# Dealing the last weights to chosen DMA engines, one output transfer, and a later load of x, in a one-core decode kernel

## The chip, the core and the metric

The kernel runs on one core of a Trainium2 chip. The core has a matrix engine (PE, with its weight loads shown apart as PEld), a vector engine (DVE), an activation engine (ACT), GpSimd (POOL) and a sync engine (SP) that here only issues transfers. Sixteen DMA engines move data between HBM and the on-chip memory (SBUF, 128 partitions). A transfer is issued by an instruction on SP or ACT; it is cut into packets, and a completion semaphore counts up as its engines finish.

The metric is device time in microseconds of one execution, the median of several runs. Less is better.

## What is computed

Two queries (batch of 2, one token) go through an attention block with a long cache and through a small feed-forward block, and a sigmoid gate mixes the two:

```python
g = sigmoid((x * gate_w).sum(-1))            # x: 2 x 1 x 512
q = x @ wq                                   # 512 -> 32 heads x 128
p = softmax(q . k_cache / sqrt(128))         # 2 x 32 heads, 4096 keys each
a = (p @ v_cache) @ wo                       # 4096 -> 512
b = relu(x @ w1) @ w2                        # 512 -> 1376 -> 512
out = g * a + (1 - g) * b                    # 2 x 1 x 512, bf16
```

All inputs are bf16. The two caches are 67 MB each; wq and wo are 4 MB each, w1 and w2 1.4 MB each. Every byte is read once.

## The kernel before

The program is written by hand: for each engine a list of instructions in order, with waits on counters of the other engines (`waits`) and on transfers' semaphores (`dwaits`). A wait holds everything behind it on that engine.

**Transfers.** SP issues nearly all of them, in this order: wq (4 MB); then the caches in 32 units of 4 MB, first four K units, then K and V in turn, then the last four V units (V12 to V15), each into one of three slots of `kv` as the unit that held the slot is done with (`freed`). Behind the third K unit stands w1 (L267), which goes into the place of wq and so waits for `pe_q`, the end of the projection of q. Behind V15 come the last weights: the last 96 rows of w2 in eleven transfers (L268 and L269, cut by `W2A` into 14, 13, 12, 11, 10, 9, 8, 7, 6, 4 and 2 rows of 1 KB); wo in two halves of 2 MB (L270, L271); the first 1280 rows of w2 in three pieces (L272, L273; 512, 512 and 256 KB). The output leaves in two transfers of 1 KB (`out_row`, L274 and L275), row 0 from SP (L277) and row 1 from ACT (L508); SP waits for both (L278). ACT issues x and gate_w (L259, L260) as its first two instructions.

**Front.** PE transposes x and gate_w (L283), DVE copies them (L286, L288, L289), PE makes the gate's sum (L293) and then q (L320), DVE and ACT spread q out (L333 to L351). POOL meanwhile sets constants: `ones32`, `ident16`, `xTw` (L219), `qbuf` (L220), others, and last `ptm` (L241). 

**Body.** For each of 64 quarter-units of K, DVE turns it (L380) and PE multiplies (L396). Each 16 of them close a softmax group; POOL copies its result into `ptm` (L425, waits for `c_ptm`), PE multiplies with V (L442), DVE collects (L453, L456). The feed-forward's hidden row `hT` is made once in between (L361, L367, L370).

**End.** After V15, PE gathers (L472, L480), DVE writes `oW` (L483), and `project` and `ffn_f` (both by `fin_row`, L488) accumulate the output in PSUM: for each of 32 rows of wo and 11 of w2 four products of 128 columns, one into each band of 32 output partitions, two partitions used in each. wo's first half is waited for at r = 0, its second at r = 16; then w2's last 96 rows, and its three pieces. DVE copies the result to `out_sb` (L507), and the two output transfers take partitions 0, 32, 64, 96 and 1, 33, 65, 97.

Of the kernel before, what the change touches and what calls it, by code (L numbers as in the profile page):

```python
# [3 lines left out]
dt = mybir.dt  # L4
# [8 lines left out]

NSLOT = 3
NKT = 3
W2A = ((0, 14), (14, 27), (27, 39), (39, 50), (50, 60), (60, 69), (69, 77), (77, 84), (84, 90), (90, 94), (94, 96))


class _Marker:
# [67 lines left out]
def bass_gated_mix__gqa_block_cached__dense_activation_relu__decode_kernel(  # L87
# [33 lines left out]
    wreg = sb("wreg", [128, 16384], dt.bfloat16)  # L121
    w2 = sb("w2", [128, 11, 512], dt.bfloat16)
# [18 lines left out]
    s4 = sb("s4", [32, 4, 128], dt.bfloat16)  # L141
    X2 = sb("X2", [128, 2, 8, 128], dt.float32)
    O_sb = sb("O_sb", [32, 2, 128], dt.bfloat16)
    oW = sb("oW", [128, 32, 2], dt.bfloat16)
    hT = sb("hT", [128, 11, 2], dt.bfloat16)
    out_sb = sb("out_sb", [128, 128], dt.bfloat16)

    PSF = nc.alloc_psum_tensor("PS", [128, 4096], dt.float32)
# [4 lines left out]
    def psf(p0, p1, c0, n):  # L153
        return PSF[p0:p1, c0:c0 + n]
# [8 lines left out]
    H_C0 = MISC + 72  # L163
    L_C0 = MISC + 96
    O_C0 = MISC + 128
    R_C0 = MISC + 256
    FIN_C0 = 0
# [4 lines left out]
    sem = {n: nc.alloc_semaphore("sem_" + n) for n in names}  # L172
# [29 lines left out]
    def pool(fn, waits=(), signal=None):  # L202
        P.add("pool", fn, waits=[marker(w) for w in waits], signal=marker(signal) if signal else None)

    def dve(fn, waits=(), signal=None, dwaits=()):
        P.add("dve", fn, waits=[marker(w) for w in waits], signal=marker(signal) if signal else None, dwaits=dwaits)

    def act(fn, waits=(), signal=None, dwaits=()):
        P.add("act", fn, waits=[marker(w) for w in waits], signal=marker(signal) if signal else None, dwaits=dwaits)

    def pe(fn, waits=(), signal=None, dwaits=()):
        P.add("pe", fn, waits=[marker(w) for w in waits], signal=marker(signal) if signal else None, dwaits=dwaits)
# [5 lines left out]
         waits=["c_i16z"], signal="c_i16")  # L218
# [13 lines left out]
         waits=["c_s1"], signal="c_s2")  # L232
    pool(lambda g: g.affine_select(out=sell[:, 16:32], in_=sell[:, 16:32], pattern=[[8, 4], [32, 4]],
                                   compare_op=ALU.is_ge, fill=0.0, base=7, channel_multiplier=-1),
         waits=["c_s2"], signal="c_sell")
# [3 lines left out]
         waits=["c_s4z"], signal="c_s4")  # L239
    pool(lambda g: g.memset(selx[:], 0.0), signal="c_selx")  # L240
    pool(lambda g: g.memset(ptm[:], 0.0), signal="c_ptm")  # L241


    wq_in = A_wq.rearrange("(p t) n -> p (t n)", t=4)
    w1_in = B_w1.rearrange("(p t) f -> p (t f)", t=4)
    wo_in = A_wo.rearrange("(p r) n -> p (r n)", r=32)
# [9 lines left out]
    def sp(fn, waits=(), dwaits=()):  # L256
        P.add("sp", fn, waits=waits, dwaits=dwaits)

    act(lambda e: e.dma_start(x_sb[0:2, :], A_x.rearrange("b s d -> (b s) d")).then_inc(sem["x"], 16))  # L259
    act(lambda e: e.dma_start(x_sb[2:3, :], gate_w.rearrange("(o d) -> o d", o=1)).then_inc(sem["gw"], 16))  # L260
    sp(lambda e: e.dma_start(wreg[:, :], wq_in).then_inc(sem["wq"], 16))
    for n, what in enumerate(order):
        waits = [freed(order[n - NSLOT])] if n >= NSLOT else []
        sp(lambda e, what=what: e.dma_start(kv[:, slot_of(what), :], unit_in(what)).then_inc(sem_slot[slot_of(what)], 16),  # L264
           waits=waits)
        if n == 2:
            sp(lambda e: e.dma_start(wreg[:, 0:5504], w1_in).then_inc(sem["w1"], 16), waits=[marker("pe_q")])  # L267
    for p0, p1 in W2A:  # L268
        sp(lambda e, p0=p0, p1=p1: e.dma_start(w2[p0:p1, 10, :], B_w2[1280 + p0:1280 + p1, :]).then_inc(sem["w2a"], 16))  # L269
    sp(lambda e: e.dma_start(wreg[:, 0:8192], wo_in[:, 0:8192]).then_inc(sem["wo0"], 16), waits=[marker("pe_h")])  # L270
    sp(lambda e: e.dma_start(wreg[:, 8192:16384], wo_in[:, 8192:16384]).then_inc(sem["wo1"], 16))  # L271
    for name, r0, r1 in (("w2b", 0, 4), ("w2c", 4, 8), ("w2d", 8, 10)):  # L272
        sp(lambda e, name=name, r0=r0, r1=r1: e.dma_start(w2[:, r0:r1, :], w2a_in[:, r0:r1, :]).then_inc(sem[name], 16))  # L273
    def out_row(e, b):  # L274
        return e.dma_start(out[b:b + 1].rearrange("b s (c n) -> (b s c) n", n=128), out_sb[b::32, :]).then_inc(sem["out"], 16)  # L275

    sp(lambda e: out_row(e, 0), waits=[marker("dve_out")])  # L277
    sp(lambda e: e.wait_ge(sem["out"], 32))  # L278


    def gate():
# [82 lines left out]

    def ffn_relu():
        for b in range(2):
            dve(lambda v, b=b: v.tensor_scalar(out=hT[:, 0:10, b], in0=PSF[:, H_C0 + b:H_C0 + 20:2], scalar1=0.0,  # L367
                                               scalar2=gm[:, b:b + 1], op0=ALU.max, op1=ALU.mult),
                waits=["pe_h", "dve_gm"])
            dve(lambda v, b=b: v.tensor_scalar(out=hT[0:96, 10, b:b + 1], in0=psf(0, 96, H_C0 + 20 + b, 1), scalar1=0.0,  # L370
                                               scalar2=gm[0:96, b:b + 1], op0=ALU.max, op1=ALU.mult),
                waits=["pe_h", "dve_gm"], signal=f"dve_h{b}")

# [47 lines left out]
    def sm_spread(g):  # L421
        dve(lambda v: v.transpose(out=ET_sb[:, :], in_=E_sb[:, :]),  # L422
            waits=[f"act_exp{g}"] + ([f"pool_pt{g - 1}_3"] if g else []), signal=f"dve_et{g}")
        for hq in range(4):
            pool(lambda e, g=g, hq=hq: e.tensor_copy(  # L425
                out=ptm[32 * hq:32 * hq + 32, g % 2, :, :, :, hq, :],
                in_=ET_sb[32 * hq:32 * hq + 32, :].rearrange("p (r u a c) -> p r u a c", r=16, u=4, a=2)),
                waits=[f"dve_et{g}", "c_ptm"] + ([f"pe_v_{4 * g - 5}"] if g >= 2 else []), signal=f"pool_pt{g}_{hq}")


    def v_unit(v):
# [38 lines left out]
    def o_gather(b):  # L470
        for u in range(8):
            pe(lambda e, u=u, b=b: e.matmul(psf(0, 32, O_C0, 128), lhsT=selx[:, 28 - 4 * u:60 - 4 * u], rhs=X2[:, b, u, :],  # L472
                                            start=(u == 0), stop=(u == 7)),
               waits=[f"dve_x{8 * b + u}_3"] + ([f"dve_rinv{b}", "dve_selx"] if u == 0 else []),
               signal=(f"pe_O{b}" if u == 7 else None))
        dve(lambda v, b=b: v.tensor_scalar(out=O_sb[:, b, :], in0=psf(0, 32, O_C0, 128), scalar1=rinv[:, b:b + 1],
                                           scalar2=gb[0:32, b:b + 1], op0=ALU.mult, op1=ALU.mult),
            waits=[f"pe_O{b}", f"dve_rinv{b}", "dve_g"], signal=f"dve_O{b}")
        for dq in range(4):
            pe(lambda e, dq=dq, b=b: e.matmul(psf(0, 128, R_C0 + 32 * b, 32), lhsT=s4[:, dq, :], rhs=O_sb[:, b, 32 * dq:32 * dq + 32],  # L480
                                              start=(dq == 0), stop=(dq == 3), tile_position=(0, 0)),
               waits=([f"dve_O{b}", "c_s4"] if dq == 0 else []), signal=(f"pe_R{b}" if dq == 3 else None))
        dve(lambda v, b=b: v.tensor_copy(out=oW[:, :, b], in_=psf(0, 128, R_C0 + 32 * b, 32)), waits=[f"pe_R{b}"], signal=f"dve_oW{b}")  # L483


    def fin_row(r, first, last, lhsT, rhs, dw, waits, signal):
        for c in range(4):
            pe(lambda e, c=c: e.matmul(psf(32 * c, 32 * c + 2, FIN_C0, 128), lhsT=lhsT, rhs=rhs[:, c * 128:(c + 1) * 128],  # L488
                                       start=first, stop=last, tile_position=(0, 32 * c), skip_group_check=True),
               dwaits=(dw if c == 0 else []), waits=(waits if c == 0 else []), signal=(signal if c == 3 else None))  # L490

    def project():
        dve(lambda v: v.memset(psf(0, 128, FIN_C0, 128), 0.0), waits=["act_exp2"], signal="dve_fin0")
        for r in range(32):
            dw = {0: [(sem["wo0"], 16)], 16: [(sem["wo1"], 16)]}.get(r, [])
            fin_row(r, r == 0, False, oW[:, r, :], wreg[:, r * 512:(r + 1) * 512], dw,
                    ["dve_oW0", "dve_oW1", "act_exp3", "dve_fin0"] if r == 0 else [], None)

    def ffn_f():
        for n, r in enumerate([10, *range(10)]):  # L500
            m = 96 if r == 10 else 128
            dw = {10: [(sem["w2a"], 16 * len(W2A))], 0: [(sem["w2b"], 16)], 4: [(sem["w2c"], 16)], 8: [(sem["w2d"], 16)]}.get(r, [])
            fin_row(r, False, r == 9, hT[0:m, r, :], w2[0:m, r, :], dw, ["dve_h0", "dve_h1"] if n == 0 else [],
                    "pe_fin" if r == 9 else None)

    def store():
        dve(lambda v: v.tensor_copy(out=out_sb[:, :], in_=psf(0, 128, FIN_C0, 128)), waits=["pe_fin"], signal="dve_out")  # L507
        act(lambda e: out_row(e, 1), waits=["dve_out"])  # L508


    gate()
# [7 lines left out]
    for i in range(64):  # L519
# [7 lines left out]
        if i % 16 == 0 and i:  # L527
            g = i // 16 - 1
# [5 lines left out]
        if i >= 19 and i % 4 == 3:  # L534
            v = i // 4 - 4
# [50 lines left out]
```

## Time and profile before

| | |
|---|---|
| three runs | 347.56, 347.62, 348.02 us; median 347.62 |
| profiled execution | 347.98 us in all; span from first to last instruction 346.5 us |
| HBM read over the span | 145.43 MB, 420 GB/s |
| PE, DVE, ACT, POOL busy | 203.3, 182.4, 13.9, 20.9 us |
| waits of SP before a unit of the caches | 245.2 us for DVE, 28.4 us for PE |
| V15, last unit: issued, landed | 303.51, 329.09 us |

The span is what the profiler sees of the core's instructions; the time of the execution has 1.48 us more around it.

The trace also has every DMA packet, with queue, start, length and bytes. It has no engine number, but an engine's packets follow one another without a gap (each begins some 4 ns before the end of the one before), so the packets can be strung into sixteen chains. The eleven transfers of w2's last rows tell the chains apart: the chains hold 11, 11, 10, 10, 9, 9, 8, 7, 6, 5, 4, 3, 2, 1, 0 and 0 packets of 1 KB, just what comes about if a transfer of n rows (n up to 16) puts one row on each of the first n engines. So the chain with 8 such packets is engine 6, and so on; 0|1, 2|3, 4|5 and 14|15 are pairs that this does not separate. Ends of the work on each chain, in us from the start of the span, and the times at which a packet of another queue (an instruction fetch of 16 KB, or of 8 KB where marked) stood between its packets:

| engine | end of V15 | w2's last rows | wo, first half | wo, second half | last piece of w2 | fetch at |
|---|---|---|---|---|---|---|
| 0 or 1 | 326.36 | 326.90 | 332.62 | 337.49 | 340.70 | |
| 0 or 1 | 326.44 | 326.97 | 332.83 | 337.69 | 340.88 | |
| 2 or 3 | 326.18 | 326.66 | 332.20 | 337.07 | 340.28 | |
| 2 or 3 | 328.33 | 328.82 | 334.47 | 339.34 | 342.49 | 110.1, 299.3 (8 KB) |
| 4 or 5 | 326.36 | 326.79 | 332.36 | 337.23 | 340.44 | |
| 4 or 5 | 328.04 | 328.48 | 334.20 | 339.07 | 342.22 | 100.5 |
| 6 | 328.01 | 328.40 | 333.98 | 338.84 | 342.00 | 140.6 |
| 7 | 326.29 | 326.63 | 332.14 | 337.03 | 340.23 | |
| 8 | 326.77 | 327.07 | 332.18 | 337.06 | 340.27 | |
| 9 | 327.88 | 328.12 | 333.13 | 338.02 | 341.21 | 178.1 |
| 10 | 327.81 | 328.00 | 333.00 | 337.88 | 341.08 | 216.9 |
| 11 | 328.00 | 328.14 | 333.15 | 338.04 | 341.24 | 257.1 |
| 12 | 328.20 | 328.30 | 333.28 | 338.17 | 341.36 | 294.9 |
| 13 | 328.63 | 328.68 | 335.17 | 340.06 | 343.23 | 40.7, 333.0 |
| 14 or 15 | 328.13 | none | 333.13 | 338.01 | 341.21 | 70.3 |
| 14 or 15 | 326.83 | none | 331.94 | 336.82 | 340.04 | |

A semaphore's count shows some 0.4 us after the packet that ends the work: the last piece of w2 is complete for PE at 343.65. Packet lengths in the stream are 1213 ns for 32 KB, 612 for 16 KB, 159 for 4 KB, 84 for 2 KB, 46 for a row of 1 KB and 9 for the write to a semaphore.

### The profile page before, as it was taken

Reading aid. Unit: us, or ns where it says so; the run is one execution under the profiler, and the core shown is the slowest. Engines: PE = TensorE matmul, PEld = TensorE weight load, DVE = VectorE, ACT = ScalarE, POOL = GpSimd, SP = SyncE. Lnnn points to the kernel's source line nnn. Section 1 sums busy time; section 2 is a strip of 40 time slices with the busy share of each in tenths; the row PEclk is TensorE's granted clock in tenths of the full one; section 3 lists DMA queues with packets and bytes.
Section 4 is the critical chain, followed back from the end, with each engine's and each line's share of the span. In section 5 each row is a group of like instructions: output and inputs, shape, how many; then the busy total and the mean of one; then the engine's idle time right before and its main releaser. Section 6 shows DMA issues by size and latency. Waiting matters only on the chain.

```text
span 346.5 us, 3037 instructions
## 1 busy us (share of the span) xinstructions
PE 203.3 (59%) x1334; PEld 76.7 (22%) x1334; DVE 182.4 (53%) x177; ACT 13.9 (4%) x48; POOL 20.9 (6%) x36
## 2 busy tenths in 40 slices
PE   0419959773755729175855839074785839422283
PEld 0203333221211203021221313021421213110052
DVE  0848877990917356391918355391648367211120
ACT  1030000000000000000000000000000000000000
POOL 8400000020000000020000000020000000200000
PEclk9967978999685958789695969789696969666576
DMA  8999999999999999999999999999999999999993
GB/s 322 446 431 431 404 453 443 427 429 424 424 426 436 443 431 431 429 424 431 435 429 439 431 435 424 422 431 435 439 426 443 427 424 431 423 435 435 395 412 154
DMA packets 5842, 145.61 MB, mean 420 GB/s; under 512 B 739, under 2 KB 838, under 8 KB 1222
## 3 DMA queue, kind: packets, MB, share of 16 engines
q1 hardware_dynamic: 5816, 145.43, 98.1%
q8 instruction: 10, 0.16, 0.2%
q14 instruction: 2, 0.02, 0.0%
q10 hardware_dynamic: 14, 0.00, 0.0%
HBM read 145.43 MB, written 0.00 MB: 420 GB/s over the span
## 4 chain that ended last, share of the span: by engine, by line
DMA 70%; DVE 14%; PE 12%; SPq 2%; issue 1%; DVEq 0%
DMA kv<-in_A_k_cache_dram 53%; DVE kt L380 11%; DMA w<-in_B_w_dram 10%; PE PS L396 8%; DMA kv<-in_A_v_cache_dram 8%; PE PS L442 4%; SPq L269 1%; DVE X L456 1%; DVE mpad L406 1%; DVE ET L422 1%; PE PS L488 0%; SPq L264 0%; DVE X L453 0%; DVE mrow L408 0%; DVE mmax L409 0%
## 5 line engine op out<-in xcount | busy, mean ns | idle before, releaser
L396 PE MATMUL PS<-kt,qbuf 128*128 128x512 bf16 x512 | 149.8, 446 | 93.9 <-DVE kt L380 93.7
L380 DVE STREAM_TRANSPOSE kt<-kv 128x2048 f32<-128x2048 f32 x64 | 144.0, 2285 | 102.8 <-DMA kv<-in_A_k_cache_dram 102.2
L396 PEld LDWEIGHTS PS<-kt,qbuf 128*128 128x128 bf16 x512 | 50.5, 108 | 190.3 <-DVE kt L380 117.8
L442 PE MATMUL PS<-kv,ptm 128*16 128x512 bf16 x512 | 37.2, 442 | 23.0 <-DMA kv<-in_A_v_cache_dram 23.0
L425 POOL COPY ptm<-ET 32x512 bf16<-32x512 bf16 x16 | 9.7, 607 | 276.5 <-DVE ET L422 275.8
L442 PEld LDWEIGHTS PS<-kv,ptm 128*16 128x16 bf16 x512 | 12.8, 98 | 45.8 <-issue 35.7
L453 DVE TENSOR_SCALAR X<-PS,maskc 128x128 f32<-128x128 f32 x16 | 5.1, 319 | 30.9 <-PE PS L442 30.9
L456 DVE SCALAR_TENSOR_TENSOR X<-PS,maskc,X 128x128 f32<-128x128 f32 x48 | 16.8, 351 | 1.7
L351 ACT ACTIVATE qbuf<-PS 32x4 bf16<-32x4 bf16 x32 | 5.7, 178 | 110.7 <-PE PS L396 110.1
L417 ACT ACTIVATE E<-PS,negm 128x512 bf16<-128x512 f32 x4 | 2.7, 687 | 154.5 <-DVE negm L413 154.5
L472 PE MATMUL PS<-X,selx 128*32 128x128 f32 x32 | 5.3, 336 | 0.0
L283 PE MATMUL PS<-ident,x_sb 3*128 3x3 bf16 x4 | 0.3, 168 | 8.1 <-DMA x_sb<-in_gate_w_dram 8.1
L361 PE MATMUL PS<-xT,wreg 128*128 128x2 bf16 (+1 forms) x44 | 2.8, 200 | 3.6 <-DMA wreg<-in_B_w_dram 3.6
L472 PEld LDWEIGHTS PS<-X,selx 128*32 128x32 f32 x32 | 4.4, 142 | 1.9 <-issue 1.4
L286 DVE COPY xT<-PS 128x12 bf16<-128x12 bf16 x1 | 0.2, 169 | 8.4 <-PE PS L283 8.4
L488 PE MATMUL PS<-wreg,oW 128*2 128x128 bf16 x128 | 2.6, 242 | 3.4 <-DMA wreg<-in_A_wo_dram 3.0
L220 POOL MEMSET qbuf<- 128x5120 bf16 x1 | 4.4, 4370 | 0.0
L507 DVE CAST out_sb<-PS 128x128 bf16<-128x128 f32 x1 | 0.3, 291 | 7.6 <-PE PS L488 7.6
L288 DVE COPY xTw<-xT 128x8 bf16<-128x8 bf16 x1 | 3.9, 3862 | 0.0
L406 DVE TENSOR_REDUCE mpad<-PS 128x1 f32<-128x512 f32 x4 | 2.7, 676 | 2.1 <-PE PS L396 2.1
L361 PEld LDWEIGHTS PS<-xT,wreg 128*128 128x128 bf16 (+1 forms) x44 | 2.7, 161 | 4.1 <-DMA wreg<-in_B_w_dram 4.1
L289 DVE TENSOR_TENSOR xg<-xT 128x8 f32<-128x8 bf16 x1 | 3.6, 3629 | 0.0
(58 smaller groups left out, 40.5 us busy)
## 6 DMA issues: line engine op xcount, KB each, us to landing
kv<-in_A_k_cache_dram SPq DMA_DIRECT2D x16, 4096.0 KB, 26.2
kv<-in_A_v_cache_dram SPq DMA_DIRECT2D x16, 4096.0 KB, 18.7
wreg<-in_A_wq_dram SPq DMA_DIRECT2D x1, 4096.0 KB, 12.4
wreg<-in_A_wo_dram SPq DMA_DIRECT2D x2, 2048.0 KB, 29.9
wreg<-in_B_w_dram SPq DMA_DIRECT2D x1, 1376.0 KB, 27.3
w<-in_B_w_dram SPq DMA_DIRECT2D x2, 512.0 KB, 33.4
w<-in_B_w_dram SPq DMA_DIRECT2D x1, 256.0 KB, 33.9
x_sb<-in_A_x_dram ACTq DMA_DIRECT2D x1, 2.0 KB
```

Of the source, the lines that this page charges most:

```text
L220: pool(lambda g: g.memset(qbuf[:], 0.0), signal="c_qbuf")
L288: dve(lambda v: v.tensor_copy(out=xTw[:, :, 0:2], in_=xT), waits=["dve_xT", "c_xTw"], signal="dve_xTw")
L351: act(lambda a, out=out, src=src: a.activation(out=out, in_=src, func=ACT.Copy), waits=[f"pe_sc_{4 * uh + 3}"], signal=f"q_1_{uh}_{hq}")
L361: return e.matmul(psf(0, m, H_C0 + 2 * ft, 2), lhsT=cols, rhs=xT3[:, t, 0:2], start=(t == 0), stop=(t == 3))
L380: dve(lambda v: v.transpose(out=dst, in_=pairs[:, :, 32 * k:32 * k + 32, :]), waits=([f"pe_sc_{i - NKT}"] if i >= NKT else []), dwaits=([s ...
L396: pe(lambda e, j=j, pos=pos, c=c, cc=cc: e.matmul(psf(0, 128, (g % 2) * BANK, 512), lhsT=qbuf[:, u % 8, j, 32 - pos:160 - pos], rhs=kt16[: ...
L406: dve(lambda v, g=g: v.tensor_reduce(out=mpad[:, 0:1], in_=psf(0, 128, (g % 2) * BANK, 512), axis=AX.X, op=ALU.max), waits=[f"pe_sc_{16 * ...
L425: pool(lambda e, g=g, hq=hq: e.tensor_copy(out=ptm[32 * hq:32 * hq + 32, g % 2, :, :, :, hq, :], in_=ET_sb[32 * hq:32 * hq + 32, :].rearra ...
L442: pe(lambda e, n=n, t=t, a=a, r16=r16, grp=grp, u4=u4, rows=rows: e.matmul(psf(32 * t, 32 * t + 16, V_B * BANK, 512), lhsT=ptm[:, grp % 2, ...
L453: dve(lambda e, src=src, dst=dst: e.tensor_scalar(out=dst, in0=src, scalar1=maskc[:, 0:1], scalar2=None, op0=ALU.mult), waits=[f"pe_v_{v}" ...
L456: dve(lambda e, src=src, dst=dst, c=c: e.scalar_tensor_tensor(out=dst, in0=src, scalar=maskc[:, c:c + 1], in1=dst, op0=ALU.mult, op1=ALU.add),
L472: pe(lambda e, u=u, b=b: e.matmul(psf(0, 32, O_C0, 128), lhsT=selx[:, 28 - 4 * u:60 - 4 * u], rhs=X2[:, b, u, :], start=(u == 0), stop=(u ...
```

## The change

- The last 96 rows of w2 go in two transfers, of 92 and 4 rows, in place of eleven. 92 rows are dealt to four engines.
- wo's first half goes in three transfers in place of one: the first 4 KB of 104 partitions (dealt to 13 engines), the same of the other 24 partitions (12 engines), and the remaining 12 KB of all 128 partitions (16 engines). `project` waits for all three.
- `oW` and `hT` get 32 columns for each row, of which 0 and 16 are used and the rest stays zero; the products take 17 columns of weights, and the two batch rows land 16 partitions apart. The output then is every 16th partition of `out_sb` and leaves in one transfer from SP; ACT issues none.
- POOL sets `hT` and `oW` to zero behind `ptm`, and the copies into `ptm` wait for the last of these.
- ACT issues x, and with it gate_w, only when POOL has set `xTw`.

```diff
-W2A = ((0, 14), (14, 27), (27, 39), (39, 50), (50, 60), (60, 69), (69, 77), (77, 84), (84, 90), (90, 94), (94, 96))
+W2A = ((0, 92), (92, 96))
+WO_A = 2048
...
-    oW = sb("oW", [128, 32, 2], dt.bfloat16)
-    hT = sb("hT", [128, 11, 2], dt.bfloat16)
+    oW = sb("oW", [128, 32, 32], dt.bfloat16)
+    hT = sb("hT", [128, 11, 32], dt.bfloat16)
...
     pool(lambda g: g.memset(ptm[:], 0.0), signal="c_ptm")
+    pool(lambda g: g.memset(hT[:], 0.0), signal="c_hT")
+    pool(lambda g: g.memset(oW[:], 0.0), signal="c_oW")
...
-    act(lambda e: e.dma_start(x_sb[0:2, :], A_x.rearrange("b s d -> (b s) d")).then_inc(sem["x"], 16))
+    act(lambda e: e.dma_start(x_sb[0:2, :], A_x.rearrange("b s d -> (b s) d")).then_inc(sem["x"], 16), waits=["c_xTw"])
...
-    sp(lambda e: e.dma_start(wreg[:, 0:8192], wo_in[:, 0:8192]).then_inc(sem["wo0"], 16), waits=[marker("pe_h")])
+    for n, (p0, p1, c0, c1) in enumerate(((0, 104, 0, WO_A), (104, 128, 0, WO_A), (0, 128, WO_A, 8192))):
+        sp(lambda e, p0=p0, p1=p1, c0=c0, c1=c1: e.dma_start(wreg[p0:p1, c0:c1], wo_in[p0:p1, c0:c1]).then_inc(sem["wo0"], 16),
+           waits=([marker("pe_h")] if n == 0 else []))
...
-    def out_row(e, b):
-        return e.dma_start(out[b:b + 1].rearrange("b s (c n) -> (b s c) n", n=128), out_sb[b::32, :]).then_inc(sem["out"], 16)
-    sp(lambda e: out_row(e, 0), waits=[marker("dve_out")])
-    sp(lambda e: e.wait_ge(sem["out"], 32))
+    sp(lambda e: e.dma_start(out.rearrange("b s (c n) -> c (b s) n", n=128),
+                             out_sb[0::16, :]).then_inc(sem["out"], 16),
+       waits=[marker("dve_out")])
+    sp(lambda e: e.wait_ge(sem["out"], 16))
...
-            pe(lambda e, c=c: e.matmul(psf(32 * c, 32 * c + 2, FIN_C0, 128), lhsT=lhsT, rhs=rhs[:, c * 128:(c + 1) * 128],
+            pe(lambda e, c=c: e.matmul(psf(32 * c, 32 * c + 17, FIN_C0, 128), lhsT=lhsT, rhs=rhs[:, c * 128:(c + 1) * 128],
...
-            dw = {0: [(sem["wo0"], 16)], 16: [(sem["wo1"], 16)]}.get(r, [])
-            fin_row(r, r == 0, False, oW[:, r, :], wreg[:, r * 512:(r + 1) * 512], dw,
+            dw = {0: [(sem["wo0"], 48)], 16: [(sem["wo1"], 16)]}.get(r, [])
+            fin_row(r, r == 0, False, oW[:, r, 0:17], wreg[:, r * 512:(r + 1) * 512], dw,
...
-            fin_row(r, False, r == 9, hT[0:m, r, :], w2[0:m, r, :], dw, ["dve_h0", "dve_h1"] if n == 0 else [],
+            fin_row(r, False, r == 9, hT[0:m, r, 0:17], w2[0:m, r, :], dw, ["dve_h0", "dve_h1"] if n == 0 else [],
...
-        act(lambda e: out_row(e, 1), waits=["dve_out"])
```

The writes of `hT` (in `ffn_relu`) and of `oW` (in `o_gather`) go to column `16 * b` in place of `b`, and wait for the zeroing.

More of the change, by code (lines that the diff above doesn't have):

```diff
@@ L366, in ffn_relu @@
         for b in range(2):
-            dve(lambda v, b=b: v.tensor_scalar(out=hT[:, 0:10, b], in0=PSF[:, H_C0 + b:H_C0 + 20:2], scalar1=0.0,
+            dve(lambda v, b=b: v.tensor_scalar(out=hT[:, 0:10, 16 * b], in0=PSF[:, H_C0 + b:H_C0 + 20:2], scalar1=0.0,
                                                scalar2=gm[:, b:b + 1], op0=ALU.max, op1=ALU.mult),
-                waits=["pe_h", "dve_gm"])
-            dve(lambda v, b=b: v.tensor_scalar(out=hT[0:96, 10, b:b + 1], in0=psf(0, 96, H_C0 + 20 + b, 1), scalar1=0.0,
+                waits=["pe_h", "dve_gm", "c_hT"])
+            dve(lambda v, b=b: v.tensor_scalar(out=hT[0:96, 10, 16 * b:16 * b + 1], in0=psf(0, 96, H_C0 + 20 + b, 1), scalar1=0.0,
                                                scalar2=gm[0:96, b:b + 1], op0=ALU.max, op1=ALU.mult),
@@ L427, in sm_spread @@
                 in_=ET_sb[32 * hq:32 * hq + 32, :].rearrange("p (r u a c) -> p r u a c", r=16, u=4, a=2)),
-                waits=[f"dve_et{g}", "c_ptm"] + ([f"pe_v_{4 * g - 5}"] if g >= 2 else []), signal=f"pool_pt{g}_{hq}")
+                waits=[f"dve_et{g}", "c_oW"] + ([f"pe_v_{4 * g - 5}"] if g >= 2 else []), signal=f"pool_pt{g}_{hq}")
     def v_unit(v):
@@ L482, in o_gather @@
                waits=([f"dve_O{b}", "c_s4"] if dq == 0 else []), signal=(f"pe_R{b}" if dq == 3 else None))
-        dve(lambda v, b=b: v.tensor_copy(out=oW[:, :, b], in_=psf(0, 128, R_C0 + 32 * b, 32)), waits=[f"pe_R{b}"], signal=f"dve_oW{b}")
+        dve(lambda v, b=b: v.tensor_copy(out=oW[:, :, 16 * b], in_=psf(0, 128, R_C0 + 32 * b, 32)), waits=[f"pe_R{b}", "c_oW"], signal=f"dve_oW{b}")
     def fin_row(r, first, last, lhsT, rhs, dw, waits, signal):
         for c in range(4):
-            pe(lambda e, c=c: e.matmul(psf(32 * c, 32 * c + 2, FIN_C0, 128), lhsT=lhsT, rhs=rhs[:, c * 128:(c + 1) * 128],
+            pe(lambda e, c=c: e.matmul(psf(32 * c, 32 * c + 17, FIN_C0, 128), lhsT=lhsT, rhs=rhs[:, c * 128:(c + 1) * 128],
                                        start=first, stop=last, tile_position=(0, 32 * c), skip_group_check=True),
```

## Prediction

> **What bounds the kernel now.** I read the page's DMA rows first, then the tail in short windows, the chain that ended last, the order of time, and the single packets. From the page:
>
> ```profile
> DMA  8999999999999999999999999999999999999993
> q1 hardware_dynamic: 5816, 145.43, 98.1%
> q8 instruction: 10, 0.16, 0.2%
> ```
>
> The DMA engines are busy in all slices but the first and last: the time is the stream's start, its bytes, and its end. The end in windows (last two columns: DMA share, GB/s):
>
> ```profile
> 339.00:340.00 1.00, 0.00 (x0) 0.00 (x0) 0.00 (x0) 0.00 (x0) 0.00 (x0) 1.00 0.95 379
> 340.00:341.00 1.00, 0.44 (x32) 0.44 (x36) 0.00 (x0) 0.00 (x0) 0.00 (x0) 1.00 0.73 285
> 341.00:342.00 1.00, 1.00 (x56) 1.00 (x44) 0.00 (x0) 0.00 (x0) 0.00 (x0) 0.52 0.37 139
> 342.00:343.00 1.00, 0.59 (x24) 0.29 (x12) 0.00 (x0) 0.00 (x0) 0.00 (x0) 0.50 0.11 41
> ```
>
> It is ragged. Perfect balance could gain the idle part, 0.05 + 0.27 + 0.63 + 0.89 = 1.84 us, and no more. The chain of waits at its end (start, length, what), and the output's issues in order of time:
>
> ```profile
> 309.26 33.75 DMA w<-in_B_w_dram
> 343.05 0.60 PE PS L488 x12
> 343.69 0.41 PE PS L488 x8
> 344.13 0.29 DVE out_sb L507
> ```
> ```profile
> 344.44 0.60 SPq L275 DMA_DIRECT2D out_dram<-out_sb  x1
> 344.45 0.61 ACTq L275 DMA_DIRECT2D out_dram<-out_sb  x1
> ```
>
> What ends last is a piece of w2, then eight products, a copy, the output transfers. The table of sixteen packet chains says why: engine 13 ends at 343.23, the next at 342.49. An instruction fetch stood on engine 13 at 333.0 for 1.09 us, and its next 16 KB packet took 1078 ns in place of 612: 1.55 us. Eight such fetches before had each held one engine, engine 13 at 40.7 too.
>
> **The change, part by part.**
>
> *Dealing.* A 4 KB packet takes 159 ns, less 4 of overlap: 155. Sixteen KB take 608, so 12 KB some 456. Engines 0-11 now move 8 + 2 packets of 4 KB and 8 of 12 KB: 5.20 us in place of 8 x 608 = 4.86, +0.34. Engine 12 has +0.03. Engines 13-15 have 8 x 0.456 = 3.65, -1.21. The 24 KB of w2's rows cost engines 0-3 24 x 0.042 = 1.02 (46 ns less overlap), the others nothing.
>
> Ends after, from each one's end of V15, with 0.2 for the slow first packets that even engine 14|15 shows (326.83 to 331.94 is 5.11, not 4.86): the late one of 2|3: 328.33 + 1.02 + 5.20 + 0.2 + 8.02 (its wo second half and w2 as now, 342.49 - 334.47) = 342.77. Engine 13: 343.23 - 1.21 - 0.05 = 341.97. The late one of 4|5: 328.04 + 5.40 + 8.02 = 341.46; 9: 341.36; 0|1: some 341.0. So the last packet goes from 343.23 to 342.77, and now it is 2|3 that ends it: -0.46.
>
> Unknown is what many small packets leave behind. After w2's rows, engines with 7 or more had three slow packets of 16 KB (with 11 rows: 966, 892, 840 ns, 0.86 us lost); those with 6 or fewer lose no more than the engines with none. Per row that would be 0.86 x 24/11 = 1.9 us on 2|3; per transfer (2 now, not 10) nothing; below nothing is excluded, the loss is counted from full rate. Since it doesn't grow from 0 to 6 rows I take 0.2, nearer the low end. Tail: -0.26, bounds -0.46 and +1.4.
>
> [...]
>
> *Output.* Both transfers are issued within 10 ns and last 0.60 and 0.61 us; SP's first packet starts at 345.67, ACT's at 346.03; the semaphore shows 346.08 and 346.44. Without the second, 0.36 goes. Alone, the issue may also be shorter: gate_w's alone took 0.24 against 0.54 of x beside wq. So gains of 0.30 to 0.65; lower, to nothing, if the nested pattern makes it slower by as much. Two rows per engine in place of one add 0.03 (20 ns packets). I take -0.50.
>
> *Seventeen columns.* A row of four products lasts 107 ns at the granted clock of 0.50, set by its 128 columns (the 512 of L442 take 427); the four weight loads run beside it. With 16 columns (L442) the loads follow one another by 3 ns, with 32 (L320) by 13. Four of 13 are 52, under 107 and under the 56 of full clock: hidden, but for the first row after each wait. After the last landing that is +0.05; if uncovered, 2 rows x 52 = +0.10.
>
> *x later.* `xTw` is set at 1.83, so x is issued near 1.85 rather than 0.81, gate_w behind it, then the table load and the first exponential (13.39). The front in order of time:
>
> ```profile
> 0.81 0.37 SPq L261 DMA_DIRECT2D wreg<-in_A_wq_dram  x1
> 0.81 0.54 ACTq L259 DMA_DIRECT2D x_sb<-in_A_x_dram  x1
> 8.12 0.27 PE L283 MATMUL PS<-ident,x_sb 3*128 3x3 bf16 x4 [8.12 <-DMA x_sb<-in_gate_w_dram]
> 8.63 3.86 DVE L288 COPY xTw<-xT 128x8 bf16<-128x8 bf16 x1
> 8.96 3.50 POOL L241 MEMSET ptm<- 128x4096 bf16 x1
> 25.32 11.76 PE L396 MATMUL PS<-kt,qbuf 128*128 128x512 bf16 x40 [5.43 <-DVE kt L380]
> ```
>
> The stream gains if x's issue held wq's up: wq's packets begin from 1.81 to 2.51 on the engines, x's at 1.75. Bounds: +0.05 (no gain, and x's packets later in the stream), -0.35 (the stragglers at 2.33 and 2.51 pulled in); I take -0.10. The loss is hidden: gate_w's packet waited between 32 KB packets until 6.39, its semaphore until 7.98; three more packets of 1.21 make some 11.5. DVE's copy already lasts as long as POOL's zeroing of `ptm` (ends 12.46); the two new zeroings, 1376 columns by the 4096 of `ptm`'s 3.50, add 1.2 us. q would start near 14.5 rather than 13.28. q is ready now at 21.20 (L345), and the first use, at 25.32, waits for DVE's first turn of K: 4.1 us of cover for 1.2. Beyond that, PE and DVE would be late, and K's slots, but SP has two units queued, some 19 us (a unit takes 9.7).
>
> *The rest, at nothing.* Nine issues of 0.25 to 0.46 us fewer on SP and two more: SP runs 20 us ahead of the data there, and its last issue already waits 4.9 us. The wait for `c_oW` on POOL ends near 14, the first copy into `ptm` is at 73. `hT`'s and `oW`'s wider steps: `oW` (0.20 us) is done at 336.3, wo's second half lands at 340.5.
>
> *Sum.* -0.26 - 0.50 + 0.05 - 0.10 = -0.81: the profiled 347.98 (span 346.5 and 1.48 around it) becomes 347.17. That execution is 0.36 above the median 347.62, so I expect a median of 346.8.
>
> **Rivals.**
>
> *Small packets on the late engine (slower).* If each row costs 0.077 us as after 11 rows, 2|3 ends at 342.77 + 1.9 = 344.6, +1.4, and the sum is +0.85: median 348.5. It decides from 1.0 us of loss on (then the gains are eaten). For it: seven engines lost 0.6 to 0.9 us in just that place. Against: a step between 6 and 7 rows, and so many semaphore writes then.
>
> *The output gains nothing.* If the nested single transfer takes as long as two, the sum is -0.31: 347.3, no change. For it: no such pattern in the trace; against: the second transfer's packets 0.36 behind the first's.
>
> *A fetch elsewhere.* The fetches went round eight engines; if the late one falls on 9-12, that ends near 341.4 + 1.55 = 342.95, 0.2 later than forecast: 347.0. The same engine was struck at 40.7 and 333.0, so I expect it again.
>
> *The front shows.* If x lands over 4 us later than worked out, K's first turns wait, yet the queue covers it; only what a stall has over 19 us reaches the end, so 348.5 needs one of near 21. Or the rows are dealt otherwise, to all engines: 346.6.
>
> **Chances.** About 0.2% (0.70 us, so 346.92) is what a measurement of this kernel can tell from no change. Forecast, 0.60: 0.50 under 346.92, 0.10 above. Small packets, 0.18: 0.12 slower, 0.06 within. Output gains nothing, 0.13, within. Fetch elsewhere 0.05: 0.03 within, 0.02 faster. The last two, 0.04: 0.02 slower, 0.02 faster. Faster 0.54, within 0.32, slower 0.14. Range: low, all good bounds, -0.46 - 0.65 + 0.05 - 0.35 = -1.41, and 0.3 of what could come if the 8 KB fetches, which hold up the late one of 2|3, fell elsewhere: 345.9. High: one more stall like that of 11 rows (0.86 for 0.2) and an output gain of only 0.3: +0.05, 347.7; into the first rival to 348.0.
>
> **What would show it.** Right: engine 13 ends near 342.0, a chain with 24 small packets ends last near 342.8; one output transfer lands within 1.6 us of its issue; q starts at 14 to 15 and PE's first L396 stays at 25.3. Wrong: packets of 16 KB over 800 ns behind the small ones, 4 KB packets well over 159 (shared ports), or a last piece of w2 after 343.6.

## The result, and the profile after

| | before | after |
|---|---|---|
| median of four runs each, on one chip | 347.61 us | 350.56 us (350.22 to 350.61) |
| ratio | | 1.0079, 95% interval 1.0067 to 1.0091 |
| profiled execution, span | 347.98, 346.5 us | 350.22, 348.9 us |
| last piece of w2 complete for PE | 343.65 | 346.33 |
| from the start of the last copy to the span's end | 2.4 us | 2.08 us |

The change makes the kernel slower by 0.8%. In the profiled executions the last piece of w2 comes 2.68 us later, the output's end is some 0.3 us shorter, and the front costs nothing: 2.68 - 0.3 is the span's 2.4. The medians lie further apart, 2.95 us, since the profiled execution of before was 0.37 us above its median and that of after 0.34 us below.

Where the time goes shows in the page's bandwidth row, 40 slices of the span, first of before, then of after with its queues:

```profile
GB/s 322 446 431 431 404 453 443 427 429 424 424 426 436 443 431 431 429 424 431 435 429 439 431 435 424 422 431 435 439 426 443 427 424 431 423 435 435 395 412 154
```
```profile
GB/s 323 447 428 425 414 464 421 421 423 451 436 430 418 421 443 440 438 421 421 425 449 436 432 421 425 438 436 440 425 419 428 440 451 423 418 428 436 315 381 150
...
q1 hardware_dynamic: 5885, 145.43, 98.0%
q8 instruction: 10, 0.16, 0.2%
```

Bytes and fetches are the same. The two rows run on one level up to the last three slices: there 315 stands for 395 and 381 for 412. The slice with 315 (322.7 to 331.4 us) holds the end of V15, w2's last rows and the start of wo's first half. The windows there, of before and of after (columns: window, its length, busy time and instructions of PE, weight loads, DVE, ACT and POOL, granted clock, DMA share, GB/s):

```profile
328.00:330.00 2.00, 0.77 (x8) 0.29 (x12) 0.00 (x0) 0.00 (x0) 0.00 (x0) 0.50 1.02 378
330.00:332.00 2.00, 2.00 (x24) 0.77 (x20) 0.00 (x0) 0.00 (x0) 0.00 (x0) 0.50 1.00 418
332.00:334.00 2.00, 2.00 (x15) 1.33 (x8) 1.05 (x3) 0.00 (x0) 0.00 (x0) 0.50 1.01 426
```
```profile
328.00:330.00 2.00, 0.00 (x0) 0.00 (x0) 0.00 (x0) 0.00 (x0) 0.00 (x0) 0.50 0.89 201
330.00:332.00 2.00, 1.46 (x16) 0.60 (x20) 0.00 (x0) 0.00 (x0) 0.00 (x0) 0.50 1.09 247
332.00:334.00 2.00, 2.00 (x21) 0.72 (x14) 0.00 (x0) 0.00 (x0) 0.00 (x0) 0.50 0.95 328
```

Read the last two columns together. The DMA engines are about as busy as before (0.89 to 1.09) and move 53, 59 and 77% as much. They don't wait for work; each packet takes longer. The packets say the same: in this stretch packets of 4 KB have a median of 288 ns (159 in before's stream) and rows of 1 KB 69 (46); all the packets of 12 KB, up to 338 us, have 567 (456 forecast). How many engines take part in a transfer shows in the 4-byte writes to semaphores: from 315 us on before has 216, one for each of w2's 96 rows, 112 for the last two units and five transfers on all sixteen engines, 8 for the output; after has 149, of which 112 are the same seven and 4 the output's, and the 33 left are the 4 + 4 + 13 + 12 of the dealt transfers.

The chain that ends last is the late one of engines 2|3, strung together as for the table of before:

```
step                          forecast     after
end of V15                    328.33       329.41
24 rows of w2                   1.02         1.92
8 + 2 packets of 4 KB           1.55         2.68
8 packets of 12 KB              3.65         3.80
 (slow first packets)           0.20          -
wo's second half, rest of w2    8.02         8.07
end                           342.77       345.88
```

The other engines end by some 344.4, so the end is as ragged as it was. The engine of the instruction fetch (at 335.4 here; by its packets one of 13 to 15) ends at 344.42, where 341.97 was forecast for engine 13 and 343.23 was its end before:

```profile
342.00:343.00 1.00, 0.00 (x0) 0.00 (x0) 0.00 (x0) 0.00 (x0) 0.00 (x0) 0.50 0.85 340
343.00:344.00 1.00, 0.74 (x32) 0.75 (x36) 0.00 (x0) 0.00 (x0) 0.00 (x0) 0.50 0.50 197
344.00:345.00 1.00, 1.00 (x48) 1.00 (x44) 0.00 (x0) 0.00 (x0) 0.00 (x0) 0.50 0.18 59
345.00:346.00 1.00, 0.95 (x40) 0.67 (x32) 0.00 (x0) 0.00 (x0) 0.00 (x0) 0.50 0.05 20
```

The chain of waits ends as before, later; behind it, in order of time, the copy and the one output transfer:

```profile
314.98 30.70 DMA w<-in_B_w_dram
345.73 0.61 PE PS L492 x16
346.37 0.42 PE PS L492 x8
```
```profile
346.82 0.29 DVE L511 CAST out_sb<-PS 128x128 bf16<-128x128 f32 x1 [9.39 <-PE PS L492]
347.14 0.65 SPq L279 DMA_DIRECT2D out_dram<-out_sb  x1
```

The last eight products take 0.42 us (0.41 before): there the 17 columns cost nothing. The issue of the single transfer isn't shorter than that of two (0.65 for 0.60), but the span ends some 0.3 us sooner after the copy. The front, in order of time:

```profile
1.87 0.55 ACTq L262 DMA_DIRECT2D x_sb<-in_A_x_dram  x1
...
10.45 0.26 PE L287 MATMUL PS<-ident,x_sb 3*128 3x3 bf16 x4 [10.45 <-DMA x_sb<-in_gate_w_dram]
...
14.51 1.93 PE L324 MATMUL PS<-wreg,xTw 128*32 128x512 bf16 x16
```

x is issued 1.06 us later and lands at 7.8, gate_w at 10.3 (11.5 was forecast). q starts at 14.51 in place of 13.28, and PE's first product of K at 25.40 (25.32): the delay is hidden as worked out. wq's first packets begin from 1.85 to 2.94 us on the engines (1.81 to 2.51 before): without x's issue beside it, wq's start is no earlier.

### The profile page after: what moved, and what is told of

Same layout as the page of the kernel before. It is cut to its first block, busy times and chain, and to the rows that moved or that the text cites. A ratio compares the mean times of both kernels' runs of the same rounds, so it can differ in the third digit from the quotient of the medians.

```text
span 348.9 us, 3016 instructions
## 1 busy us (share of the span) xinstructions
PE 200.0 (57%) x1318; PEld 76.5 (22%) x1334; DVE 181.3 (52%) x177; ACT 13.9 (4%) x48; POOL 22.1 (6%) x38
## 4 chain that ended last, share of the span: by engine, by line
DMA 69%; DVE 14%; PE 12%; SPq 3%; issue 1%; DVEq 0%
DMA kv<-in_A_k_cache_dram 53%; DVE kt L384 11%; DMA w<-in_B_w_dram 9%; DMA kv<-in_A_v_cache_dram 7%; PE PS L400 7%; PE PS L446 4%; SPq L278 2%; DVE X L460 1%; DVE mpad L410 1%; DVE ET L426 1%; SPq L274 0%; PE PS L492 0%; SPq L267 0%; DVE X L457 0%; DVE mrow L412 0%
## 5 line engine op out<-in xcount | busy, mean ns | idle before, releaser
L400 PE MATMUL PS<-kt,qbuf 128*128 128x512 bf16 x496 | 145.5, 443 | 96.2 <-DVE kt L384 93.5
L400 PEld LDWEIGHTS PS<-kt,qbuf 128*128 128x128 bf16 x512 | 50.2, 107 | 189.4 <-DVE kt L384 117.3
L492 PE MATMUL PS<-wreg,oW 128*17 128x128 bf16 x128 | 3.0, 265 | 5.3 <-DMA wreg<-in_A_wo_dram 5.3
L492 PEld LDWEIGHTS PS<-wreg,oW 128*17 128x17 bf16 x128 | 2.5, 113 | 5.5 <-DMA wreg<-in_A_wo_dram 4.0
L324 PE MATMUL PS<-wreg,xTw 128*32 128x512 bf16 x32 | 3.6, 628 | 0.0
```

The source lines that it names most:

```text
L400: pe(lambda e, j=j, pos=pos, c=c, cc=cc: e.matmul(psf(0, 128, (g % 2) * BANK, 512), lhsT=qbuf[:, u % 8, j, 32 - pos:160 - pos], rhs=kt16[: ...
L492: pe(lambda e, c=c: e.matmul(psf(32 * c, 32 * c + 17, FIN_C0, 128), lhsT=lhsT, rhs=rhs[:, c * 128:(c + 1) * 128], start=first, stop=last, ...
```

## The experiments

All times are medians; each ratio is to the kernel before, run beside it, with its 95% interval.

### Which part costs it

*The changed kernel with wo's first half in one transfer.*

```diff
-    for n, (p0, p1, c0, c1) in enumerate(((0, 104, 0, WO_A), (104, 128, 0, WO_A), (0, 128, WO_A, 8192))):
...
+    sp(lambda e: e.dma_start(wreg[:, 0:8192], wo_in[:, 0:8192]).then_inc(sem["wo0"], 16), waits=[marker("pe_h")])
```

> The changed kernel with wo's first half as one transfer again. In the changed kernel the 4 KB packets of wo took 200 to 480 ns in place of 159, and so did the 12 KB packets beside them (up to 1011 in place of 461). Theory A (the dealing of wo in runs of consecutive partitions makes DMA engines share what leads into a group of partitions): most of the 2.95 us goes, 347.6 to 348.4. Theory B (4 KB packets are slow in themselves there): the same time as A here; told apart by the next runs. Theory C (the 24 rows of w2 on four engines are the cost): stays at 350.0 to 350.6.

347.57 us, ratio 0.9998 (0.9989 to 1.0008), just under the range that A and B share. wo's dealing makes up 350.56 - 347.57 = 2.99 us of the changed kernel, more than its whole loss.

*The kernel before with wo's dealing alone* (the same three transfers, nothing else):

> The kernel before with the dealing of wo alone (104 and 24 partitions of 4 KB, then 12 KB of all). A and B: 349.4 to 350.6, since the loss comes with it. C: 347.0 to 347.7.

349.62 us, 1.0059 (1.0041 to 1.0077): +1.94. So it costs something by itself, and 1.05 more beside the other parts. The slow stretch goes and comes with it; first the changed kernel with wo whole, then wo's dealing alone:

```profile
328.00:330.00 2.00, 0.62 (x8) 0.29 (x12) 0.00 (x0) 0.00 (x0) 0.00 (x0) 0.50 1.02 381
```
```profile
328.00:330.00 2.00, 0.10 (x4) 0.14 (x8) 0.00 (x0) 0.00 (x0) 0.00 (x0) 0.50 1.06 218
```

*w2's last rows in two transfers, alone*, and *in one transfer on all sixteen engines*:

```diff
-W2A = ((0, 14), (14, 27), ... (94, 96))
+W2A = ((0, 92), (92, 96))       # first kernel
+W2A = ((0, 96),)                # second kernel
```

> The kernel before with w2's last 96 rows in two transfers (92 and 4) on four engines, alone. In the changed kernel the 1 KB packets grew from 46 to 60-118 ns after the tenth. Theory A (sharing by runs of consecutive partitions): the late one of engines 2 and 3 pays 24 rows of 0.046 to 0.1 us instead of ten and their 0.7 us of aftermath; engine 13 still ends last. Same time as before within 0.6 us: 347.4 to 348.3. Rival (small packets leave 0.077 us per row behind): 348.3 to 349.0, engine 2 or 3 last.

> The kernel before with the 96 rows in one transfer, six consecutive rows on each of sixteen engines. Engine 13 has five rows more, 0.25 us: 347.7 to 348.1 if rows cost 0.046 each; if runs of consecutive rows are shared and cost 0.1 each, 348.0 to 348.5. [...]

348.05 us, 1.0008 (0.9999 to 1.0017), and 348.01 us, 1.0007 (0.9998 to 1.0017), beside 347.69: at most +0.36 and +0.32, within what the measurement can tell. With 24 rows each on four engines the late one of 2|3 ends at 343.03 and engine 13 still ends last, at 343.20; with six rows each on all, engine 13 ends last at 343.60. To use all engines brings nothing here.

*x later, alone*, and *one output transfer, alone* (with the 17 columns and the zeroing):

> The kernel before with x and gate_w issued behind the first constants, alone. As forecast: 0.1 us less. As the changed kernel's landings say (wq 13.32 in place of 13.23, V13 309.55 in place of 309.44): 0.1 us more, 347.6 to 347.9; the first packets of wq start no earlier than 1.81.

> The kernel before with the output in one transfer and 17 columns, with the zeroing that goes with it; wo, w2 and x as before. From the copy of the result to the end of the span it is 2.4 us before (344.13 to 346.5) and 2.08 in the changed kernel (346.82 to 348.9): 0.3 us less, 347.1 to 347.5. If 17 columns of weights cost something, the last eight products last over 0.45 us and it is 347.4 to 347.8.

347.73 us, 0.9999 (0.9990 to 1.0007): x's time of issue is worth nothing. 347.06 us, 0.9982 (0.9973 to 0.9991): -0.63, the one part that gains, and the fastest kernel here that does the whole work. This is twice the 0.3 us that it gains behind the copy. Most of the rest lies outside the span: an execution has 1.26 to 1.31 us around the span in the five kernels with one output transfer (means of their runs), and 1.48 to 1.54 us in all those with two. Whether the number of transfers, ACT's part in them or the zeroing that comes with the change does this, no run tells apart.

*The changed kernel with w2's eleven transfers put back.* The single parts sum to +1.94 + 0.36 + 0.04 - 0.63 = +1.71, the change costs +2.9:

> The changed kernel with only w2's last 96 rows put back to the eleven transfers. If the parts simply add: 347.65 + 1.94 (wo dealt alone) + 0.04 (x) - 0.63 (output) = 349.0, and w2's dealing is worth 1.5 us beside wo's though 0.36 alone. If the parts do not act on each other it would be the changed kernel's 350.56 less 0.36: 350.2. Theory: small packets on four engines and 4 KB packets on thirteen are in the same engines one after another, and the first delays the late engine (V15's end at 329.41 in the changed kernel); so 349.0, with V15's last chain back near 328.4 to 328.8.

349.00 us, 1.0039 (1.0026 to 1.0053), as the sum without w2's part has it. So w2's dealing costs 350.56 - 349.00 = 1.6 us beside wo's, and 0.36 alone. The end of V15 did not come back as expected: its last packet ends at 329.07 there, over the 328.4 to 328.8 (329.57 in the changed kernel, 328.63 before). How the two dealings act on each other stays open.

### Small packets, or the partitions they go to

The first suspect was the shortness of the packets. *The kernel before with wo's first 4 KB and then 12 KB, each over all 128 partitions:*

```diff
+    for n, (p0, p1, c0, c1) in enumerate(((0, 128, 0, 2048), (0, 128, 2048, 8192))):
...
```

> The kernel before with wo's first half in two transfers of all 128 partitions, 4 KB and then 12 KB of each: the same packet sizes, dealt to all sixteen engines. A: no loss, 347.5 to 347.9 (8 packets of 155 ns in place of a quarter of 8 x 608 cost 0.02 us). B: a loss as in the kernel with wo dealt, 349.0 to 350.5.

*The same packets, but the 4 KB in two transfers of 64 partitions:*

```diff
+    for n, (p0, p1, c0, c1) in enumerate(((0, 64, 0, 2048), (64, 128, 0, 2048), (0, 128, 2048, 8192))):
...
```

> As the last one, but the 4 KB part in two transfers of 64 partitions (0 to 63, then 64 to 127), each on all sixteen engines with four rows per engine: packet sizes, their number per engine and the bytes per engine are the same as with 128. A: the engines now share in pairs, so 32 KB per engine go at half rate, 1.2 us more if nothing overlaps: 348.2 to 349.2, with 4 KB packets near 300 ns. [...] B: the same as with 128 partitions in one.

347.79 us, 1.0003 (0.9993 to 1.0013), and 349.44 us, 1.0050 (1.0034 to 1.0066), 0.2 us over the range that A gave it. Both move the same 128 packets of 4 KB, 8 for each of the sixteen engines on the mean. The windows of the first and of the second:

```profile
328.00:330.00 2.00, 0.84 (x12) 0.33 (x16) 0.00 (x0) 0.00 (x0) 0.00 (x0) 0.50 1.11 392
330.00:332.00 2.00, 2.00 (x24) 0.75 (x20) 0.00 (x0) 0.00 (x0) 0.00 (x0) 0.50 1.02 420
```
```profile
328.00:330.00 2.00, 0.00 (x0) 0.00 (x0) 0.00 (x0) 0.00 (x0) 0.00 (x0) 0.50 1.03 227
330.00:332.00 2.00, 1.76 (x20) 0.71 (x24) 0.00 (x0) 0.00 (x0) 0.00 (x0) 0.50 1.02 274
```

The last column decides: 392 against 227 GB/s with the same packets and bytes, at a full DMA share in both (1.11 and 1.03). 4 KB packets have a median of 167 ns in the one and 274 in the other. So neither the packets' size nor uneven loads are needed for the loss; what is left is which partitions a transfer holds. That engines share in pairs is A's premise; the run shows the longer packets, not the pairs. (The second kernel also has one transfer more; the kernels further on that move wo's first half in a single transfer settle that this isn't it.)

*wo's first half in whole rows of 16 KB, partitions 32-95 first, or 0-63 first:*

```diff
+    for n, (p0, p1, c0, c1) in enumerate(((32, 96, 0, 8192), (0, 32, 0, 8192), (96, 128, 0, 8192))):   # first kernel
...
+    for n, (p0, p1, c0, c1) in enumerate(((0, 64, 0, 8192), (64, 96, 0, 8192), (96, 128, 0, 8192))):   # second kernel
...
```

> The kernel before with wo's first half in three transfers of whole 16 KB rows: partitions 32-95, then 0-31, then 96-127. Packets stay at 16 KB, and each of the 16 engines has 4, 2 and 2 of them. Theory P (engines that write into the same places at once share a rate; in the two transfers of 64 partitions tried so far 4 KB packets took 274 ns in place of 159, a factor of 1.7): it depends on which partitions lie in one transfer. [...] Then the first piece runs at 612 ns a packet, the four packets of the others at up to 1.7 x 612 = 1040: 4 x 0.43 = +1.7 us at most, 348.0 to 349.4. Theory D (any transfer of fewer than 128 partitions is slow, wherever it lies): all 8 packets an engine slow, up to 8 x 0.43 = +3.4, and the same time as the kernel with 0-63 first. Theory F (it is the packets' shortness together with few of them a transfer): 16 KB packets at 612, and 347.7 to 348.1 for both.

> As the one before it, but the transfers are partitions 0-63, 64-95 and 96-127. Theory P: now the first piece is shared too, two engines to a place, and its packets take near 1040 ns: 348.9 to 351.1, some 1.7 us over the other kernel, and under 300 GB/s while the first piece is moved. Theory D: as slow as the other kernel, within 0.3 us. Theory F: both near 347.9.

351.59 us, 1.0110 (1.0095 to 1.0126), and 353.60 us, 1.0173 (1.0159 to 1.0187). The difference of 2.0 us is near the 1.7 that Theory P gave it, but both are over its ranges, by 2.2 and 2.5 us. That the first piece is unshared from 32 and shared by two engines from 0 was the author's assumption, and no trace shows it. In part the ranges failed because of the factor of 1.7; the windows of 32-95 first and of 0-63 first show 2:

```profile
328.00:330.00 2.00, 0.55 (x8) 0.29 (x12) 0.00 (x0) 0.00 (x0) 0.00 (x0) 0.50 1.07 370
...
332.00:334.00 2.00, 2.00 (x26) 1.64 (x18) 1.13 (x4) 0.00 (x0) 0.00 (x0) 0.94 1.02 213
```
```profile
328.00:330.00 2.00, 0.00 (x0) 0.00 (x0) 0.00 (x0) 0.00 (x0) 0.00 (x0) 0.50 1.01 181
...
332.00:334.00 2.00, 2.00 (x24) 0.79 (x20) 0.00 (x0) 0.00 (x0) 0.00 (x0) 0.50 1.02 221
```

The 64 partitions from 32 go at nearly the full rate (370 GB/s for 378 before; 16 KB packets 675 ns at the median), the 64 from 0 at half (181 GB/s, 1422 ns), and transfers of 32 partitions at half in both (213 GB/s from 332 to 334 us in the first, 221 and 213 from 334 to 338 in the second).

The two kernels also differ in the rows of wo that they read first. *The crossings: partitions 0-63 filled from rows 32-95, and 32-95 from rows 0-63* (these kernels sum over permuted rows of wo):

```diff
+    for n, (p0, p1, q0, q1) in enumerate(((0, 64, 32, 96), (64, 96, 0, 32), (96, 128, 96, 128))):   # first kernel
+    for n, (p0, p1, q0, q1) in enumerate(((32, 96, 0, 64), (0, 32, 64, 96), (96, 128, 96, 128))):   # second kernel
+        sp(lambda e, ...: e.dma_start(wreg[p0:p1, 0:8192], wo_in[q0:q1, 0:8192]) ...   # both
```

> Three transfers as in the two kernels with 64, 32 and 32 partitions, but partitions 0-63 are filled from rows 32-95 of wo, 64-95 from rows 0-31, 96-127 from their own: the sums come out over permuted rows of wo, and nothing else differs, in bytes, packets and waits. Of the two kernels, that with 32-95 first took 351.59 us with packets of 675 ns (median) in 328 to 330 us, that with 0-63 first 353.60 us with 1422 ns there. Theory P (the places in the SBUF that are written to decide): as 0-63 first, 353.3 to 353.9, first packets over 1200 ns. Rival H (the rows of wo in HBM that are read decide, since the two first pieces also differ in these): as 32-95 first, 351.3 to 351.9, first packets near 675 ns.

> The other crossing: partitions 32-95 filled from rows 0-63 of wo, 0-31 from rows 64-95, 96-127 from their own (again permuted rows of wo). Theory P: as 32-95 first, 351.3 to 351.9, first packets near 675 ns. Rival H: as 0-63 first, 353.3 to 353.9, over 1200 ns.

353.79 us, 1.0178 (1.0163 to 1.0194), and 351.26 us, 1.0103 (1.0086 to 1.0120). In 328 to 330 us, partitions 0-63, then 32-95:

```profile
328.00:330.00 2.00, 0.00 (x0) 0.00 (x0) 0.00 (x0) 0.00 (x0) 0.00 (x0) 0.50 0.88 160
```
```profile
328.00:330.00 2.00, 0.38 (x4) 0.14 (x8) 0.00 (x0) 0.00 (x0) 0.00 (x0) 0.50 1.19 365
```

The places written in the SBUF decide (353.79 for 353.60 with 0-63 first, 351.26 for 351.59 with 32-95 first); what is read makes no difference that shows. (The median packet of the second is 840 ns in this window, not the 675 that were expected; its rate, 365, is that of the kernel it was to match, 370.)

### Whose places they are

What stayed open was the size: +3.9 us with 32-95 first, where the two transfers of 32 partitions, four packets an engine, at twice 612 ns give 4 x 0.61 = +2.4. Either a transfer of part of the partitions always loses, or only that of some partitions does. *Only partitions 32-95, or only 0-63, of wo's first half are moved* (the other 64, 1 MB, are left out):

```diff
+    for n, (p0, p1, c0, c1) in enumerate(((32, 96, 0, 8192),)):   # first kernel
...
+    for n, (p0, p1, c0, c1) in enumerate(((0, 64, 0, 8192),)):    # second kernel
...
```

> The kernel before, but of wo's first half only the rows of partitions 32-95 are moved, in one transfer; 0-31 and 96-127 (1 MB) are left out and keep older numbers. Each engine has 4 packets of 16 KB in place of 8, so without any loss the end comes 4 x 608 ns = 2.43 us earlier: 347.5 - 2.4 = 345.1. Theory O (an engine has places of its own, where only it writes in a transfer of 128 partitions; a transfer of part of them is slow only as far as it sends engines to others' places). [...] Rival Q (a transfer of part of the partitions always loses something, as the +3.9 of the three transfers, over the 1.7 that was allowed, may say): 345.8 to 347.0.

> The same with partitions 0-63 moved and 64-127 (1 MB) left out: the same bytes, packets and count. [...] Rival Q: as the kernel with 32-95, within 0.5 us.

345.10 us, 0.9929 (0.9913 to 0.9946), as counted without any loss and under Rival Q's range, and 349.19 us, 1.0044 (1.0029 to 1.0059), 4.1 us above the first, where Rival Q had 0.5 at most. The first moves half the bytes and gains all of it; the second moves the same half and is slower than the whole:

```profile
328.00:330.00 2.00, 0.58 (x8) 0.30 (x12) 0.00 (x0) 0.00 (x0) 0.00 (x0) 0.50 1.01 378
330.00:332.00 2.00, 2.00 (x28) 0.69 (x20) 0.00 (x0) 0.00 (x0) 0.00 (x0) 0.50 1.02 426
```
```profile
328.00:330.00 2.00, 0.00 (x0) 0.00 (x0) 0.00 (x0) 0.00 (x0) 0.00 (x0) 0.50 1.08 201
330.00:332.00 2.00, 1.29 (x16) 0.52 (x20) 0.00 (x0) 0.00 (x0) 0.00 (x0) 0.50 0.98 205
```

378 and 426 GB/s are the full rate (378 and 418 in the kernel before in the same windows). So a transfer of part of the partitions does not always lose: that of 32-95 costs nothing. With 0-63 16 KB packets take 1226 to 1337 ns (medians of the windows from 328 to 334 us), twice 612. Theory O allows for both, but no trace shows which engine writes which partition, so its cause, engines at others' places, stays the author's guess. Early engines seem to hold up late ones that are still in V15: its 32 KB packets took up to 2265 ns here and 2613 with 0-63 first, in place of 1213. That is the likely source of what the losses have over a plain doubling (4.1 us between the last two kernels for 2.4 by count); it wasn't measured by itself.

*The dealt wo without its 24-row part* (these 96 KB are left out) asks where in the change the loss is:

```diff
+    for n, (p0, p1, c0, c1) in enumerate(((0, 104, 0, 2048), (0, 128, 2048, 8192))):
...
```

> The kernel before with wo's first half dealt, but the second of the three transfers (the first 4 KB of partitions 104-127, 96 KB) left out: these partitions keep older numbers. [...] If the whole loss is in the 24-row part: the late engines of before keep 347.2 to 347.7, less than before since engines 13-15 have 1.2 us less to move, and 12 KB packets near 460 ns. If the 104-row part costs as well (engines that fall out of step with those on the same places): 348.3 to 349.0, 4 KB packets well over 159 ns.

348.99 us, 1.0040 (1.0025 to 1.0055), 4 KB packets at 209 to 297 ns (medians of the windows from 326 to 332 us). Already the 104-row part costs +1.48, the larger share of the 1.94. Why is not shown; what the run shows is that the 104 rows alone are slow.

### A last try

*One output transfer, and w2's last piece dealt to 104 and 24 partitions*, where most engines are done:

```diff
-    for name, r0, r1 in (("w2b", 0, 4), ("w2c", 4, 8), ("w2d", 8, 10)):
+    for name, r0, r1, p0, p1 in (..., ("w2d", 8, 10, 0, 104), ("w2d", 8, 10, 104, 128)):
```

> The kernel before with the single output transfer (347.06 alone), and w2's very last piece dealt in 104 and 24 partitions: engines 0-12 have 8 packets of 2 KB, and engines 0-11 two more; 13-15 have none. Engine 13, which ends last, is relieved of 8 x 81 = 0.65 us, and then the late one of 2 or 3 ends last, at 342.49 + 2 x 0.08 = 342.65 in place of 343.23: -0.5 at best, 346.5. Theory P: 2 KB packets of engines that lie on each other's places take up to 1.7 x 84 = 143 ns; but by then most engines have ended (340.0 to 341.4), so the late ones have their places to themselves: 346.5 to 346.8. Rival: the dealing costs here too what it costs ahead of wo's first half (early engines slow the late ones while they overlap): 347.1 to 347.6, no better than the output's change alone.

347.83 us, 1.0004 (0.9995 to 1.0013): 0.77 slower than the output's change alone, and over the rival's range too. In 340 to 342 us 4 KB packets take 212 ns and 2 KB packets 109 at the median, where the kernel with the output alone has 159 and 84. So the late packets were slowed here too, where Theory P had them at full rate. In the profiled executions the last packet of w2 ends at 343.23 us, and at 343.04 with the output alone. Whether the gain of 0.5 was there to be had, no run shows.

## Why the prediction was wrong

It said 346.8 us (345.9 to 348.0) and faster; it was 350.56 and slower. By its own steps:

- **Dealing: wrong, and this is the step that failed.** "A 4 KB packet takes 159 ns, less 4 of overlap: 155 ... Engines 0-11 ... 5.20 us" took a duration from transfers of 128 partitions and put it on transfers of 104 and 24. They hold the same bytes per packet and not the same partitions. 4 KB took 252 ns in the 104-row part on the late engine (2.02 us for 8) and 330 in the 24-row part. The same holds for "24 x 0.042 = 1.02", which was 1.92, and for the end of V15, taken as it was, which came 1.08 later. Of the 3.11 us by which the last packet is later than forecast (345.88 for 342.77), 1.13 are the 4 KB packets, 0.90 the rows and 1.08 the end of V15. The tail was -0.26 (bounds -0.46 and +1.4) and is +2.68, past the bound. What the runs showed in its place: the rate hangs on the partitions that are written (349.44 us for 347.79 with the same packets; 349.19 for 345.10 with half the bytes).
- **The range left the longer packets out.** Every packet's duration in the sum came from transfers of 128 partitions or from w2's single rows, and 4 KB packets well over 159 ns stood only among the signs of being wrong. The slower rows (+0.90) and the stretched V15 (+1.08) were in no term either. The slow packets behind w2's rows, which stood on the engines with 7 rows or more, the prediction read as a step between 6 and 7 rows; the rows themselves took 46 ns there, and no run tests this reading.
- **Who ends last: right, but not for the reason given.** The late one of 2|3 ends last, and the fetch again strikes an engine that, by its packets, is one of 13 to 15 (at 335.4 for 333.0). Taken as engine 13, that engine was not relieved: it ends at 344.42, not at 341.97, since its eight packets of 12 KB took 5.2 us in place of 3.65 and its V15 ended 0.94 later.
- **The slower rival: right in sign and engine, wrong in mechanism and size.** It put the loss into slow packets that the 24 rows leave behind. With these rows alone the kernel took 348.05, and in the changed kernel the 12 KB packets on that engine took 3.80 us for 3.65. The loss lay in the small packets themselves and in the stretched V15. It gave 348.5.
- **Output: right in size, in part by luck.** -0.50 and +0.05 for the columns; alone -0.63. Behind the copy it is only some -0.3; another 0.2 lies outside the span, where the sum took the 1.48 us as fixed.
- **x: the cover was right** (q at 14.51, PE's first L400 at 25.40), the gain of 0.10 wasn't there: +0.04, within the noise. The packets of wq that start last start 0.43 us later, not sooner (2.94 for 2.51).
- **What was to show it wrong showed it:** 4 KB packets well over 159 (252 and 330), and a last piece after 343.6 (346.33). The shared ports named beside the packets were a guess, and no trace shows a port. The two parts that were costed apart also act on each other: w2's dealing costs 0.36 alone, within the noise, and 1.6 beside wo's.

## What to carry to other kernels

The duration of a packet holds for the partitions it was measured on: before engines are given unequal shares by the number of partitions of a transfer, measure the packets of a transfer over just these partitions. In this kernel a split by columns over all 128 partitions was free (347.79 for 347.68), and so was partitions 32-95 alone (345.10 with half the bytes); 0-63 halved the rate (201 to 205 GB/s for 378 to 426). A full DMA share beside half the GB/s in a window is how such a loss looks (1.08 beside 201 with 0-63 alone, 1.01 beside 378 with 32-95 alone).

## What was not expected of the hardware

- Two transfers with the same packet sizes, counts and bytes differ by a factor of two in rate, by their first partition alone: 64 partitions from 32 at 378 to 426 GB/s, 64 from 0 at 201 to 205.
- With small pieces behind it the stream slows, so that a piece costs time before it is itself waited for: the last 32 KB packets of V15 took up to 1354 ns in the kernel before, 1622 with w2's rows dealt, 1987 with wo dealt and 2272 with both (V15's end on the late engine 329.41 for 328.33). That early engines stretch the packets of late ones is inferred from the order in time.
- Two output transfers issued within 10 ns on two queues end later than one of twice the rows: 2.4 us behind the copy against 2.08. The kernels with two also have some 0.2 us more outside the span.
